# Score products in three steps, and an exp in two bf16 tiles that VectorE multiplies

## The chip, the cores and the metric

The kernel runs on one core of one Trainium2 chip. The metric is device microseconds of one execution. The profile is of one more execution, with every instruction's start and duration. Engines are named as the profile names them: PE is TensorE's matmul, PEld its weight load, ACT is ScalarE, DVE is VectorE, POOL is GpSimd, SP is SyncE, whose queue issues nearly all DMAs.

## The reference

For x of 2048 tokens by 1024 channels, a gate mixes a linear state space model with an attention block:

```
g = sigmoid((x * gate_w).sum(-1))
a: Bu = x @ B_bar.T (complex);  h_t = Lam_bar * h_(t-1) + Bu_t;  y = 2 * Re(h @ C.T) + x * Dskip
b: q, k, v of 32 heads of 32;  softmax(q k' / sqrt(32)) v;  @ wo
out = g * a + (1 - g) * b        # bf16 in and out
```

The attention has 32 x 2048 x 2048 scores, and each needs an exponential.

## The kernel before, in words

**Bursts.** The 32 heads are taken four at a time, as 8 groups. A group has 8 units of 256 queries, a unit 8 bursts of 256 keys: 512 bursts. In a burst (`burst`, L1612) PE computes eight score products, for two key tiles (`kl`) and four heads (`h`), each 32 rows by 256 queries (L1624). They go into two of three PSUM slots, which rotate: slot `sl[0]` holds heads 0 and 1, `sl[1]` heads 2 and 3. ScalarE takes the exp of each slot, 128x1024, as one instruction (`exp`, L1643). PE then multiplies exps of the burst before by V (`pv`, L1709), and adds up to about four 512-column products of a "dense chain": projections to Q, K and V (L1426, L1445), the products with B called u (L1457), with C (L1504), and the output projection (L1535). All dense chains end in PSUM bank 7, and VectorE copies the result out (`evac`) before the next one writes there.

**Order.** It is written out beforehand. `build` (L1734) steps through the bursts and keeps a clock of its own: a burst is given `PERIOD` = 1.83 us, 0.17 less after one with a shortened exp, and VectorE's clock `dve_t` is advanced by a planned cost for each operation. VectorE's other work, the state space scan and its tables and folds (`bg`, `bg2`), is put in where it fits in front of a limit. Each engine then works through its own list in that order and waits on semaphores. A `Sched.op` with `writes` waits for all readers and writers of its token; one with `acc` waits for those on other engines only, and becomes the token's last writer.

**X tiles.** ScalarE is relieved in 92 pairs of bursts (`X_PLAN`, `X_AT`). In a burst of a pair, the last 256 columns of the second slot are not given to ScalarE, whose exp is then 128x768 (L1640). VectorE copies them from PSUM, scaled, as 32-bit fixed point numbers (`x_in`, L1633); the short exp waits for it, since both read the slot. After the pair's second x_in come the steps of `x_ops` (L1653) on 128x512: `lo`, the low 16 bits, is the fraction of the exponent, `hi` the whole part. VectorE does two polynomial steps (L1667, L1668) and a third that adds `hi` (L1664); GpSimd then scales that to the bits of a bf16 (L1665), and PE multiplies it by V (`x_pv`, L1688). `X_LAST` is both the planned cost of the third step and the mark by which the planner knows it. `x_flush` runs what is left of the steps when PE's product comes due.

**Weights.** `wb` holds Q's weights once, K's and V's for two groups in turn (`w_of`), three B tiles, and late in the run some rows of the output weights. `build` issues Q's load at burst 28 of a group, K's and V's, for the group after the next, at burst 25. The C matrix comes in as transposing DMAs from burst `C_LOADS` on, every fourth burst.

Of the kernel before, what the change touches and what calls it, by code (L numbers as in the profile page):

```python
# [6 lines left out]
BF = mybir.dt.bfloat16  # L7
# [3 lines left out]
ALU = mybir.AluOpType  # L11
# [720 lines left out]
class GpPhaseA:  # L732
# [24 lines left out]
    def first(self, name):  # L757
        return self.alias.pop(name, [])
# [164 lines left out]
GROUPS = 8  # L923
# [8 lines left out]
RING = 60  # L932
C_LOADS = 28

X_AT = ((0, 2), (4, 6), (0, 4))
X_PLAN = (64, 72, 80, 88, 92, 96, 100, 104, 108, 112, 116, 120, 124, 128, 132, 136, 144, 152, 160, 168, 172, 176, 180, 184, 188, 192, 200, 208, 216, 224, 228, 232, 236, 240, 244, 248, 252, 256, 260, 264, 272, 280, 288, 296, 304, 312, 316, 320, 324, 328, 332, 336, 344, 352, 356, 360, 364, 368, 372, 376, 380, 384, 388, 392, 396, 400, 404, 408, 412, 416, 420, 424, 428, 432, 436, 440, 444, 448, 452, 456, 460, 464, 468, 472, 476, 480, 484, 488, 492, 496, 500, 504)
X_COLS = 256
F_TS, F_ST = 1.32, 1.24
I_MM = 0.61
X_LAST = 0.735  # L940
U_LAG, U_AHEAD = 3, 32
# [17 lines left out]
class FastPath:  # L959

    def __init__(self, nc, S, es, d, flag):
# [10 lines left out]
        self.V = T("V", [128, 2, 16, 4, 33], BF)  # L972
        wb = T("wb", [128, 8192], BF)
        self.wq = wb[:, 0:1024].rearrange("p (a n) -> p a n", a=8)
        self.wkv = wb[:, 1024:5120].rearrange("p (s q a n) -> p s q a n", s=2, q=2, a=8)
        self.bT = wb[:, 5120:8192].rearrange("p (s a n) -> p s a n", s=3, a=8)

        row = lambda o, n: wb[:, o:o + 1024 * n].rearrange("p (a n) -> p a n", a=n)
        self.wo3 = [row(1024, 2), row(5120, 3), row(3072, 1), self.cT[0][:, 0:1, :], self.cT[0][:, 1:2, :]]
        self.wo = [(self.wo3[0][:, a, :], "wo0") for a in range(2)] + [(self.wo3[4][:, 0, :], "wo4")] + [(self.wo3[1][:, a, :], "wo1") for a in range(3)]  # L980
        self.wo += [(self.wo3[3][:, 0, :], "wo3"), (self.wo3[2][:, 0, :], "wo2")]
        self.pt = T("pt", [128, 6, 2, 512], BF)
# [3 lines left out]
        self.hp = hp  # L986
        self.hpx = wb[:, 5120:8192].rearrange("p (k n) -> p k n", k=6)
        ub = T("ub", [128, 2, 2, 512], BF)
# [3 lines left out]
        self.xq = T("xq", [128, 2 * X_COLS], F32)  # L992
        self.xp = T("xp", [128, 2 * X_COLS], BF)
        self.ut = T("ut", [128, 2, 512], F32)
        self.ht = T("ht", [128, 2, 512], BF)
# [69 lines left out]
    def w_of(self, g, part):  # L1065
        return (self.wkv[:, g % 2, part - 1], ("w", g % 2, part)) if part else (self.wq, ("w", 0, 0))

# [544 lines left out]
    def burst(self, B):  # L1612
# [5 lines left out]

        def mm(e):
            m = None  # L1620
            for kl in range(2):
                for h in range(4):
                    kt = 2 * i + kl
                    m = e.matmul(ps[:, 2 * sl[h // 2] + h % 2, 256 * kl:256 * (kl + 1)], K[32 * h:32 * h + 32, g % 2, 128 * kt:128 * (kt + 1)],  # L1624
                                 Q[32 * h:32 * h + 32, qz, qo:qo + 256], start=True, stop=True, tile_position=(32 * h, 0))
# [27 lines left out]
    def x_ops(self, b):  # L1653

        xi, xq, xp = self.xi[:, b % 2], self.xq, self.xp
        lo = xi.bitcast(mybir.dt.uint16)[:, 0::2]
        hi = xi.bitcast(mybir.dt.int16)[:, 1::2]
        bits = xp.bitcast(mybir.dt.int16)[:]
        w = 65536.0
        i2, p2 = [("xi", b % 2, 0), ("xi", b % 2, 1)], [("xp", 0), ("xp", 1)]  # L1660

        def last():
            assert self.x_out == len(self.x_done)
            self.dve(lambda e: e.scalar_tensor_tensor(xq[:], hi, 128.0 / X_K, xq[:], ALU.mult, ALU.add), i2 + ["xq"], ["xq"], "x_q")  # L1664
            self.pool(lambda e: e.tensor_scalar(bits, xq[:], X_K, 128.0 * (E0 + 126.0), ALU.mult, ALU.add), ["xq"], p2, "x_p")  # L1665
            self.x_done.add(b)
        return [(0.73, 0.0, lambda: self.dve(lambda e: e.scalar_tensor_tensor(xq[:], lo, E2 / E3 * w, lo, ALU.add, ALU.mult), i2, ["xq"], "x_q")),  # L1667
                (0.73, 0.0, lambda: self.dve(lambda e: e.scalar_tensor_tensor(xq[:], xq[:], E1 / E3 * w * w, lo, ALU.add, ALU.mult), ["xq"] + i2, ["xq"], "x_q")),  # L1668
                (X_LAST, 0.0, last)]
# [64 lines left out]
    def build(self):  # L1734
# [8 lines left out]
        for m in range(3):  # L1743
            self.ld_b(m)
        for part in (1, 2):
            self.ld_w(1, part)
        self.plan()
        self.pt_own = {}
        self.x_of, self.x_batch, self.x_when = {}, [], {}
        self.xbg, self.x_done, self.x_out = [], set(), 0  # L1750
        self.opening()
# [32 lines left out]
        first = FIRST  # L1784
        wo1 = wo6 = last = False
        nal = nc = 0
# [3 lines left out]
        for p in range(first, NBURST):  # L1790
# [40 lines left out]

            if pg == 25 and g + 2 < GROUPS:
                assert g or not (proj[0] or cur and cur.tag == "proj")
                for part in (1, 2):
                    self.ld_w(g + 2, part)
            if pg == 28 and g + 1 < GROUPS:
                assert not (cur and cur.tag == "proj")
                self.ld_w(g + 1, 0)
            wsv = self.d["B_wo"].rearrange("(a p) n -> p a n", p=128)
            if p == 386:  # L1840
                self.dma(lambda e: e.dma_start(self.wo3[0], wsv[:, 0:2, :]), [], ["wo0"] + [("w", 0, q) for q in (1, 2)], "ld_wo")
            if not cs and cur is None and not wo1 and self.c_left[3] == 0:
                wo1 = True
                self.dma(lambda e: e.dma_start(self.wo3[1], wsv[:, 3:6, :]), [], ["wo1"] + [("bT", r) for r in range(3)] + [("hp", 8, k) for k in range(6)], "ld_wo")
            if g >= 6 and not wo6 and not cs and self.c_left[3] == 0:
                wo6 = True
                self.dma(lambda e: e.dma_start(self.wo3[3], wsv[:, 6:7, :]), [], ["wo3", ("cT", 0, 0), ("cTf", 0, 0, 0), ("cTf", 0, 0, 1)], "ld_wo")
                self.dma(lambda e: e.dma_start(self.wo3[4], wsv[:, 2:3, :]), [], ["wo4", ("cT", 0, 1), ("cTf", 0, 1, 0), ("cTf", 0, 1, 1)], "ld_wo")
            if g >= 6 and not last and not proj[7] and not us and not cs and cur is None and not self.bg:

                last = True
                xs = [("xr", r) for r in range(16)]
                assert wo1 and wo6
                self.dma(lambda e: e.dma_start(self.wo3[2], wsv[:, 7:8, :]), [], ["wo2"] + [("w", 1, q) for q in (1, 2)] + xs, "ld_wo")
            if g >= 6 and not cs and self.c_left[3] == 0 and nal < 8 and p > self.c_end:
# [50 lines left out]
            while self.xbg or self.bg or self.bg2:  # L1906
# [40 lines left out]
                if c > 0:  # L1947
                    self.dve_t = now + c
            if ended is not None:
                ended.evac()  # L1950
                self.dve_t = max(self.dve_t, dense_end) + 0.65
# [4 lines left out]
    def tail(self):  # L1956
# [41 lines left out]
        for r in range(2):  # L1998
            for cb in range(2):
                bank = 2 + r + 2 * cb  # L2000
                w = dict(acc=[("tb", bank)]) if cb == 0 else dict(writes=[("tb", bank)] + ([("S", 2)] if r == 0 else []), **({} if r == 0 else dict(acc=[("S", 2)])))
                S.op("pe", lambda e, r=r, cb=cb, bank=bank: e.matmul(ps[:, bank, :], OT[:, 7, 1792 + 128 * r:1920 + 128 * r], wo[7][0][:, 512 * cb:512 * (cb + 1)],
                                                                    start=(cb == 1), stop=True), reads=[("OT", 7, 7, r), "wo2"], name="tail", **w)
            if r == 0:
# [131 lines left out]
```

## Time and profile before

| | |
|---|---|
| median of 3 runs | 926.67 us (926.38 to 930.31) |
| the profiled execution | 928.11 us, its span from first to last instruction 926.3 us |
| granted TensorE clock, mean | 0.996 |
| busy, of the span | PE 902.5, ACT 907.3, DVE 758.4, POOL 86.8 us |
| full exps, short exps | 840, 184 |
| DMA | 77.69 MB, mean 84 GB/s |

A group of the profile reads: line, engine, operation, out<-in by the program's names, shapes, count | busy us, mean ns of one | idle time just before, and what ended it. A row of the timeline reads: start, duration, engine, line, operation, count, and in brackets the idle time before it with its releaser. A row of the stretches gives busy time of PE, PEld, DVE, ACT and POOL with counts, then clock, DMA share and GB/s. A row of the waits gives the total, the number and the longest. Consecutive operations of an engine can overlap: the next one's start can lie before the end of the one before.

### The profile page before, as it was taken

Reading aid. Unit: us, or ns where it says so; the run is one execution under the profiler, and the core shown is the slowest. Engines: PE = TensorE matmul, PEld = TensorE weight load, DVE = VectorE, ACT = ScalarE, POOL = GpSimd, SP = SyncE. Lnnn points to the kernel's source line nnn. Section 1 sums busy time; section 2 is a strip of 40 time slices with the busy share of each in tenths; the row PEclk is TensorE's granted clock in tenths of the full one; section 3 lists DMA queues with packets and bytes.
Section 4 is the critical chain, followed back from the end, with each engine's and each line's share of the span. In section 5 each row is a group of like instructions: output and inputs, shape, how many; then the busy total and the mean of one; then the engine's idle time right before and its main releaser. Section 6 shows DMA issues by size and latency. Waiting matters only on the chain.

```text
span 926.3 us, 33979 instructions
## 1 busy us (share of the span) xinstructions
PE 902.5 (97%) x15316; PEld 503.9 (54%) x15316; DVE 758.4 (82%) x1310; ACT 907.3 (98%) x1034; POOL 86.8 (9%) x156
## 2 busy tenths in 40 slices
PE   8899999999999999999999999999999999999996
PEld 4554754557555565546655565555655655445553
DVE  2788989998989999989989999899988655776665
ACT  6999999999999999999999999999999999999996
POOL 2000000111000101011111020000010010001010
PEclk9999999999999999999999999999999999999998
DMA  9569747750457101272012511413001112424312
GB/s 195 87 116 184 93 84 138 144 116 5 81 113 152 50 20 49 67 147 53 19 51 65 126 45 31 104 63 103 20 15 43 31 51 77 156 83 128 114 62 75
DMA packets 170934, 77.69 MB, mean 84 GB/s; under 512 B 147232, under 2 KB 155424, under 8 KB 170784
## 3 DMA queue, kind: packets, MB, share of 16 engines
q1 hardware_dynamic: 168624, 74.94, 36.3%
q8 instruction: 121, 1.98, 0.9%
q10 hardware_dynamic: 2160, 0.53, 0.3%
q14 instruction: 29, 0.24, 0.1%
HBM read 25.18 MB, written 20.97 MB: 50 GB/s over the span
## 4 chain that ended last, share of the span: by engine, by line
PE 52%; ACT 40%; DVE 4%; DMA 2%; SPq 1%; issue 1%; POOL 0%; DVEq 0%; ACTq 0%
ACT f_pt L1643 32%; PE f_ps L1709 14%; PE f_ps L1624 10%; PE f_ps L1426 9%; PE f_ps L1504 7%; PE f_ps L1457 6%; ACT f_pt L1640 5%; PE f_ps L1445 5%; SPq L1062 1%; ACT f_cT L1643 1%; PE f_ps L1688 1%; DMA f_xT<-in_A_x_dram 1%; ACT f_Et L1643 1%; DMA f_wb<-in_A_B_im_dram 1%; DMA f_ub<-u_scratch 0%
## 5 line engine op out<-in xcount | busy, mean ns | idle before, releaser
L1643 ACT ACTIVATE f_pt<-f_ps 128x1024 bf16<-128x1024 f32 x760 | 728.8, 1090 | 1.5 <-PE f_ps L1624 1.3
L1709 PEld LDWEIGHTS f_ps<-f_V,f_pt 128*128 128x128 bf16 x7184 | 222.2, 96 | 95.3 <-issue 68.7
L1709 PE MATMUL f_ps<-f_V,f_pt 128*128 128x33 bf16 x7184 | 258.0, 178 | 0.0
L1624 PE MATMUL f_ps<-f_Q,f_K 32*128 32x256 bf16 x4096 | 203.3, 273 | 10.8 <-ACT f_pt L1643 3.3
L1640 ACT ACTIVATE f_pt<-f_ps 128x768 bf16<-128x768 f32 x184 | 165.3, 898 | 0.7 <-PE f_ps L1624 0.6
L1624 PEld LDWEIGHTS f_ps<-f_Q,f_K 32*128 32x128 bf16 x4096 | 60.7, 92 | 148.0 <-ACT f_pt L1643 120.6
L1457 PE MATMUL f_ps<-f_xT,f_wb 128*128 128x512 bf16 x512 | 131.5, 379 | 1.6 <-DMA f_wb<-in_A_B_im_dram 0.7
L1665 POOL TENSOR_SCALAR f_xp<-f_xq 128x512 int16<-128x512 f32 x92 | 67.3, 732 | 646.0 <-DVE f_xq L1664 471.3
L1426 PE MATMUL f_ps<-f_xT,f_wb 128*128 128x512 bf16 x464 | 119.3, 379 | 0.1
L1633 DVE TENSOR_SCALAR f_xi<-f_ps 128x256 int32<-128x256 f32 x184 | 77.4, 421 | 17.6 <-PE f_ps L1624 13.3
L1362 DVE TENSOR_TENSOR_SCAN f_ht<-f_pf,f_init,f_ut 128x512 bf16<-128x512 f32 x64 | 81.3, 1279 | 0.0
L1504 PE MATMUL f_ps<-f_cT,f_hp 128*128 128x512 bf16 x272 | 74.5, 379 | 0.1
L1667 DVE SCALAR_TENSOR_TENSOR f_xq<-f_xi 128x512 f32<-128x512 uint16 x92 | 63.7, 692 | 3.2
L1668 DVE SCALAR_TENSOR_TENSOR f_xq<-f_xq,f_xi 128x512 f32<-128x512 f32 x92 | 63.6, 692 | 3.1
L1664 DVE SCALAR_TENSOR_TENSOR f_xq<-f_xi,f_xq 128x512 f32<-128x512 int16 x92 | 63.5, 690 | 2.6
L1457 PEld LDWEIGHTS f_ps<-f_xT,f_wb 128*128 128x128 bf16 x512 | 40.1, 96 | 40.5 <-issue 8.6
L1535 PE MATMUL f_ps<-f_wb,f_OT 128*128 128x512 bf16 x188 | 61.2, 381 | 0.4 <-DVE f_Et L1547 0.4
L1445 PE MATMUL f_ps<-f_wb,f_xT 128*128 128x128 bf16 x896 | 59.3, 219 | 0.0
L1426 PEld LDWEIGHTS f_ps<-f_xT,f_wb 128*128 128x128 bf16 x464 | 36.1, 96 | 35.6 <-issue 7.6
L1461 DVE CAST f_ub<-f_ps 128x512 bf16<-128x512 f32 x64 | 44.1, 688 | 10.4 <-PE f_ps L1457 9.7
L1445 PEld LDWEIGHTS f_ps<-f_wb,f_xT 128*128 128x128 bf16 x896 | 50.4, 97 | 3.8 <-issue 3.8
L1722 DVE RECIPROCAL f_rc<-f_ps 128x8 f32<-128x8 f32 x63 | 13.1, 207 | 47.6 <-PE f_ps L1688 43.5
(149 smaller groups left out, 822.5 us busy)
## 6 DMA issues: line engine op xcount, KB each, us to landing
u_scratch<-f_ub SPq DMA_DIRECT2D x64, 128.0 KB, 2.1
f_ub<-u_scratch SPq DMA_DIRECT2D x32, 256.0 KB, 3.0
ag_scratch<-f_Ag SPq DMA_DIRECT2D x32, 256.0 KB, 2.0
f_hp<-ag_scratch SPq DMA_DIRECT2D x32, 256.0 KB, 3.0
f_wb<-in_B_wqkv_dram SPq DMA_DIRECT2D x21, 256.0 KB, 4.1
out_dram<-f_xT SPq DMA_DIRECT2D x16, 256.0 KB, 2.2
f_OT<-f_On SPq DMA_TRANSPOSE x63, 2.3
f_wb<-in_B_wo_dram SPq DMA_DIRECT2D x1, 768.0 KB
```

The lines of the kernel that those rows point to most:

```text
L1362: ops.append((1.24, lambda ri=ri: dve(lambda e: e.tensor_tensor_scan(ht[:, ri, :], rr, ut[:, ri, :], self.init[:, ri, j:j + 1], ALU.mult, ...
L1426: mms.append((1, lambda e, f, l, a=a, w=w: e.matmul(ps[:, bank, :], w[:, a, :], xT[:, a, 512 * ch:512 * (ch + 1)], start=f, stop=l), [tok] ...
L1445: m = e.matmul(ps[:, bank, 128 * q:128 * (q + 1)], xT[:, a, 128 * kt:128 * (kt + 1)], w[:, a, :], start=(a == 0), stop=(a == 7))
L1457: mms.append((1, lambda e, f, l, a=a: e.matmul(ps[:, 7, :], bT[:, (2 * n + ri) % 3, a, :], xT[:, a, 512 * ch:512 * (ch + 1)], start=f, sto ...
L1504: mms.append((1, lambda e, f, l, j=j, ri=ri, h=h: e.matmul(ps[:, 7, :], h[:, cols], cT[ri][:, j, 512 * cb:512 * (cb + 1)], start=f, stop=l ...
L1624: m = e.matmul(ps[:, 2 * sl[h // 2] + h % 2, 256 * kl:256 * (kl + 1)], K[32 * h:32 * h + 32, g % 2, 128 * kt:128 * (kt + 1)], Q[32 * h:32 ...
L1633: first = self.dve(lambda e: e.tensor_scalar(self.xi[:, b % 2, X_COLS * n:X_COLS * (n + 1)], ps[:, 2 * s + 1, 512 - X_COLS:512], X_A, X_LO ...
L1640: self.S.op("act", lambda e: e.activation(flat(self.tile[p]), flat(ps[:, 2 * s:2 * s + 2, :]), ACT.Exp, scale=SCALE), reads=[("S", s)], wr ...
L1643: self.act(lambda e: e.activation(self.tile[p], ps[:, 2 * s:2 * s + 2, :], ACT.Exp, scale=SCALE), [("S", s)], [("pt", p)], "exp")
L1665: self.pool(lambda e: e.tensor_scalar(bits, xq[:], X_K, 128.0 * (E0 + 126.0), ALU.mult, ALU.add), ["xq"], p2, "x_p")
L1667: return [(0.73, 0.0, lambda: self.dve(lambda e: e.scalar_tensor_tensor(xq[:], lo, E2 / E3 * w, lo, ALU.add, ALU.mult), i2, ["xq"], "x_q") ...
L1709: m = e.matmul(ps[:, 6, o:o + 33], self.tile[p][:, h2, 256 * kl + 128 * qt:256 * kl + 128 * (qt + 1)], V[:, g % 2, 2 * i + kl, h, :], star ...
```

## The change

- The eight score products of a burst become three operations of PE: two products that write the first slot, four that end the first slot and begin the second, two that end the second. The order of the products stays.
- `x_ops`: VectorE's third step goes. GpSimd makes two bf16 tiles, `xe` (two to the whole part, from `hi`) beside the first step and `xm` (the polynomial's value) after the second; VectorE multiplies them into `xp`. The multiplication is planned at 0.36 and not before 0.9 us (`X_GAP`) after the step before it.
- The list of pairs loses 92 and 100 and gains 268, 276, 284, 292, 300 and 308: 96 pairs.
- K's and V's weights have one buffer each; K's and V's for the next group are loaded at a group's first burst (K's for group 1 at burst 17), Q's at burst 38 (`W_AT`). Projections may start four bursts later.
- C is loaded from burst 32 on. The output weights go to rows of the C and B tiles, seven loads at once when the C chains are done, and the last row later.

```diff
-C_LOADS = 28
+C_LOADS = 32
+W_AT = (38, 0, 17)
-X_LAST = 0.735
+X_LAST = 0.36
-X_K = 128.0 * E3 / 65536.0 ** 3
+X_K = E3 / 65536.0 ** 3
+X_GAP = 0.9
...
+        self.wqkv = [wb[:, 1024 * k:1024 * (k + 1)].rearrange("p (a n) -> p a n", a=8) for k in range(3)]
...
-        def mm(e):
+        def mm(e, some):
...
-        self.S.op("pe", mm, reads=[("K", g % 2, i // 2), ("Q", qz)], writes=[("S", sl[0]), ("S", sl[1])], name="qk")
+        s0, s1 = ("S", sl[0]), ("S", sl[1])
+        for some, kw in ((((0, 0), (0, 1)), dict(writes=[s0])),
+                         (((0, 2), (0, 3), (1, 0), (1, 1)), dict(writes=[s1], acc=[s0])),
+                         (((1, 2), (1, 3)), dict(acc=[s1]))):
+            self.S.op("pe", lambda e, some=some: mm(e, some), reads=[("K", g % 2, i // 2), ("Q", qz)], name="qk", **kw)
...
+        def first():
+            self.dve(lambda e: e.scalar_tensor_tensor(xq[:], lo, E2 / E3 * w, lo, ALU.add, ALU.mult), i2, ["xq"], "x_q")
+            self.pool(lambda e: e.tensor_scalar(bits, hi, 128.0, 128.0 * 127.0, ALU.mult, ALU.add), i2, ["xe"], "x_e")
+
+        def second():
+            self.dve(lambda e: e.scalar_tensor_tensor(xq[:], xq[:], E1 / E3 * w * w, lo, ALU.add, ALU.mult), ["xq"] + i2, ["xq"], "x_q")
+            self.pool(lambda e: e.tensor_scalar(self.xm[:], xq[:], X_K, E0, ALU.mult, ALU.add), ["xq"], ["xm"], "x_m")
+
         def last():
-            self.dve(lambda e: e.scalar_tensor_tensor(xq[:], hi, 128.0 / X_K, xq[:], ALU.mult, ALU.add), i2 + ["xq"], ["xq"], "x_q")
-            self.pool(lambda e: e.tensor_scalar(bits, xq[:], X_K, 128.0 * (E0 + 126.0), ALU.mult, ALU.add), ["xq"], p2, "x_p")
+            self.dve(lambda e: e.tensor_tensor(xp[:], self.xm[:], self.xe[:], ALU.mult), ["xm", "xe"], p2, "x_p")
...
-                proj[g][8 + c].after = max(16 * c, 32)
+                proj[g][c].after = W_AT[1] + 4
+                proj[g][8 + c].after = max(16 * c, W_AT[0] + 4)
...
-            if pg == 25 and g + 2 < GROUPS:
-                for part in (1, 2):
-                    self.ld_w(g + 2, part)
-            if pg == 28 and g + 1 < GROUPS:
+            if pg == W_AT[1 if g else 2] and g + 1 < GROUPS:
+                self.ld_w(g + 1, 1)
+                if g:
+                    self.ld_w(g + 1, 2)
+            if pg == W_AT[0] and g + 1 < GROUPS:
                 self.ld_w(g + 1, 0)
...
-                    if c == X_LAST and self.x_out != len(self.x_done):
+                    if c == X_LAST and (xs or now < self.x_ready or self.x_out != len(self.x_done)):
...
+                if i:
+                    self.x_ready = self.dve_t + X_GAP
```

More of the change, by code (lines that the diff above doesn't have):

```diff
@@ L1065, in w_of @@
     def w_of(self, g, part):
-        return (self.wkv[:, g % 2, part - 1], ("w", g % 2, part)) if part else (self.wq, ("w", 0, 0))
+        return self.wqkv[part], ("w", 0, part)
     def ld_w(self, g, part, eng="sp"):
@@ L1617, in burst @@
         qz, qo = (4 * g + qb // 2) % 5, 256 * (qb % 2)
-        def mm(e):
+        def mm(e, some):
             m = None
[L1621 to L1625, printed above, removed]
-            return m
-        self.S.op("pe", mm, reads=[("K", g % 2, i // 2), ("Q", qz)], writes=[("S", sl[0]), ("S", sl[1])], name="qk")
+            for kl, h in some:
+                kt = 2 * i + kl
+                m = e.matmul(ps[:, 2 * sl[h // 2] + h % 2, 256 * kl:256 * (kl + 1)], K[32 * h:32 * h + 32, g % 2, 128 * kt:128 * (kt + 1)],
+                             Q[32 * h:32 * h + 32, qz, qo:qo + 256], start=True, stop=True, tile_position=(32 * h, 0))
+            return m
+        s0, s1 = ("S", sl[0]), ("S", sl[1])
[3 more added lines that the diff above has]
+            self.S.op("pe", lambda e, some=some: mm(e, some), reads=[("K", g % 2, i // 2), ("Q", qz)], name="qk", **kw)
         mine = self.x_of.get(B)
@@ L1744, in build @@
             self.ld_b(m)
-        for part in (1, 2):
-            self.ld_w(1, part)
+        self.ld_w(1, 2)
         self.plan()
@@ L1784, in build @@
         first = FIRST
-        wo1 = wo6 = last = False
+        wo1 = last = False
         nal = nc = 0
@@ L1838, in build @@
+            if pg == W_AT[0] and g + 1 < GROUPS:
+                assert not proj[0]
                 self.ld_w(g + 1, 0)
             wsv = self.d["B_wo"].rearrange("(a p) n -> p a n", p=128)
-            if p == 386:
-                self.dma(lambda e: e.dma_start(self.wo3[0], wsv[:, 0:2, :]), [], ["wo0"] + [("w", 0, q) for q in (1, 2)], "ld_wo")
-            if not cs and cur is None and not wo1 and self.c_left[3] == 0:
+            if not wo1 and not cs and cur is None and self.c_left[3] == 0:
@@ L1843, in build @@
                 wo1 = True
[L1844 to L1848, printed above, removed]
+                for a in range(7):
+                    j = a if a < 3 else a - 3
+                    x = [("cT", 0, j), ("cTf", 0, j, 0), ("cTf", 0, j, 1)]
+                    if a in (3, 4, 5):
+                        x = [("bT", a - 3)] + [("hp", 8, k) for k in (2 * a - 6, 2 * a - 5)]
+                    self.dma(lambda e, a=a: e.dma_start(self.wo[a][0], wsv[:, a, :]), [], ["wo%d" % a] + x, "ld_wo")
@@ L1849, in build @@
             if g >= 6 and not last and not proj[7] and not us and not cs and cur is None and not self.bg:
                 last = True
-                xs = [("xr", r) for r in range(16)]
-                assert wo1 and wo6
-                self.dma(lambda e: e.dma_start(self.wo3[2], wsv[:, 7:8, :]), [], ["wo2"] + [("w", 1, q) for q in (1, 2)] + xs, "ld_wo")
+                assert wo1
+                self.dma(lambda e: e.dma_start(self.wo[7][0], wsv[:, 7, :]), [], ["wo7", ("cT", 0, 4), ("cTf", 0, 4, 0), ("cTf", 0, 4, 1)], "ld_wo")
```

32 lines of the change are left out of this document (14 added, 18 removed).

## The prediction, made before the result was known

> **What bounds the kernel now.** I read the page first, then the stretches, the chain of waits, and last the timeline around single pairs.
>
> ```profile
> span 926.3 us, 33979 instructions
> PE 902.5 (97%) x15316; PEld 503.9 (54%) x15316; DVE 758.4 (82%) x1310; ACT 907.3 (98%) x1034; POOL 86.8 (9%) x156
> ```
>
> PE at 97% and ACT at 98% look alike. A PE row counts matmuls whose ends are modelled, so ACT has to be asked separately: is it ever without work?
>
> ```profile
> 25.00:900.00 875.00, 864.26 (x14833) 483.22 (x14826) 737.19 (x1244) 871.79 (x991) 80.76 (x132) 1.00 0.36 81
> 650.00:675.00 25.00, 25.00 (x495) 17.21 (x494) 22.88 (x40) 25.00 (x30) 2.47 (x4) 1.00 0.07 18
> ```
>
> The columns are PE, PEld, DVE, ACT and POOL busy time. Between 25 and 900 us ACT is idle for 875 - 871.79 = 3.2 us in all. So ACT carries the time, and anything that doesn't shorten its own work can return only little. The chain of waits shows its beat:
>
> ```profile
> 258.69 6.42 ACT f_pt L1643 x7
> 265.11 0.70 ACT f_pt L1640
> L1643 ACT ACTIVATE f_pt<-f_ps x760: 1018/1103/1309, 9.9 to 916.1; 128x1024 bf16<-128x1024 f32 x190
> L1640 ACT ACTIVATE f_pt<-f_ps 128x768 bf16<-128x768 f32 x184 | 165.3, 898 | 0.7 <-PE f_ps L1624 0.6
> ```
>
> Seven full exps take 6.42 us, 0.917 each; one shortened by an x tile takes 0.70. (Each lasts over 1 us, since the next starts before it ends.) The first exp starts at 9.9 and the last at 916.1, 906.2 us apart. The 1024 exps, 184 of them short, need 839 x 0.917 + 184 x 0.70 = 898.2 between those starts. So 8.0 us are lost to waits of every kind: 3.2 as idle ACT after 25 us, and an estimated 4.8 in the opening and in starts late by less than the overlap. Those 8.0 are all that the score step, DVE and the DMAs could give back.
>
> **Four more pairs.** 92 pairs become 96, so eight exps shrink from 0.917 to 0.70: 8 x 0.217 = **-1.7 us**. This lies on the path and is the surest term.
>
> **Score products in three steps.** Today all eight wait until both slots are free:
>
> ```profile
> PEld f_ps L1624 <- ACT f_pt L1643: 120.6, 312, 1.0
> 402.67 0.12 PEld L1624 LDWEIGHTS f_ps<-f_Q,f_K 32*128 32x128 bf16 x8 [0.42 <-ACT f_pt L1643]
> 402.68 0.40 PE L1624 MATMUL f_ps<-f_Q,f_K 32*128 32x256 bf16 x8
> L1624 PE MATMUL f_ps<-f_Q,f_K x4096: 264/268/278, 9.5 to 914.7; 32*128 32x256 bf16 x196
> ```
>
> One product lasts 0.268 and eight 0.40, so they run as two rounds of four, 0.13 apart. The first step needs only slot 0, which the exp before last left. It can run ahead of ACT, and then the second step holds the two others of the first round beside the first two of the next. The first exp is released after the sixth product, not the eighth: at best 0.13 earlier. That counts only in bursts where PE stood waiting for ACT (312), and there ACT has work in hand anyway; what helps is that PE starts its values and dense products 0.13 sooner, and the next burst is less often late. Where PE arrives late by itself nothing changes. Bounds: 0 (ACT is covered) and half of the 4.8, 2.4. I take a quarter, **-1.2 us**, since much of the 4.8 stands in the opening, where PE is behind. A gain is not excluded by any row, and neither is a small loss for one more wait per burst; no row prices that, so I put it at nothing, covered by the same 0.13.
>
> **Weights and C later.** The one large idle stretch of ACT is this:
>
> ```profile
> 65.46 1.29 SPq L1081 DMA_TRANSPOSE f_cT<-in_A_C_re_dram  x1
> 66.79 1.30 SPq L1081 DMA_TRANSPOSE f_cT<-in_A_C_im_dram  x1
> 68.14 1.28 SPq L1071 DMA_DIRECT2D f_wb<-in_B_wqkv_dram  x1
> 69.53 0.67 SPq L1474 DMA_DIRECT2D f_ub<-u_scratch  x1
> 73.34 0.69 DVE L1353 TENSOR_TENSOR f_ht<-f_ub,f_Et 128x1024 bf16<-128x1024 bf16 x1 [2.39 <-DMA f_ub<-u_scratch]
> 75.27 0.57 PE L1709 MATMUL f_ps<-f_V,f_OT 128*128 128x33 bf16 x16 [1.24 <-DVE f_On L1723]
> 77.36 1.94 ACT L1643 ACTIVATE f_OT<-f_ps 128x1024 bf16<-128x1024 f32 x2 [1.34 <-PE f_ps L1624]
> ```
>
> Burst 28 issues the first pair of C transposes and Q's weights. Both stand ahead of the load of u at 69.53; VectorE sits 2.39 us for it, PE waits 1.24 for the normalisation queued behind on VectorE, and ACT loses 1.34. The change moves C to burst 32 and Q's weights to 38, so the load has a free queue. A later load of u then meets C instead, where VectorE may have other work or not. Bounds 0 and -1.34; I take **-0.8**.
>
> K's and V's weights have one buffer now and are loaded at a group's first burst (K for group 1 at burst 17).
>
> ```profile
> f_wb<-in_B_wqkv_dram SPq DMA_DIRECT2D x21, 256.0 KB, 4.1
> ```
>
> They land in 4.1 us, and no product may use them for four bursts, at least 4 x 1.62 = 6.5 us by the exps above (one full, one short). SP then holds u's stores and B's transposes behind two loads instead of at burst 25: the same queueing at another place, nothing net. If the cover went, a dense chain would wait perhaps 1 us, seven times at most. The output weights become seven single loads at one moment and an eighth later; the output chains still start at burst 442 at the earliest, behind the last projections, so nothing.
>
> **VectorE and GpSimd.** Per pair the third VectorE pass over 512 float32 elements goes, and a bf16 product comes. GpSimd does two passes instead of one: the exponent tile as soon as the pair's second x_in is done, the mantissa tile after the second VectorE pass.
>
> ```profile
> 292.26 0.42 DVE L1633 TENSOR_SCALAR f_xi<-f_ps 128x256 int32<-128x256 f32 x1
> 292.72 0.69 DVE L1667 SCALAR_TENSOR_TENSOR f_xq<-f_xi 128x512 f32<-128x512 uint16 x1
> 293.44 0.69 DVE L1668 SCALAR_TENSOR_TENSOR f_xq<-f_xq,f_xi 128x512 f32<-128x512 f32 x1
> 402.84 0.42 DVE L1353 TENSOR_TENSOR f_Ag<-f_tq,f_ut 128x512 bf16<-128x512 bf16 x1
> 296.17 0.68 DVE L1664 SCALAR_TENSOR_TENSOR f_xq<-f_xi,f_xq 128x512 f32<-128x512 int16 x1
> 296.76 0.69 DVE L1353 TENSOR_TENSOR f_ht<-f_ub,f_Et 128x1024 bf16<-128x1024 bf16 x1
> 296.93 1.00 POOL L1665 TENSOR_SCALAR f_xp<-f_xq 128x512 int16<-128x512 f32 x1 [15.61 <-DVE f_xq L1664]
> 297.37 1.10 DVE L1353 TENSOR_TENSOR f_tq<-f_ub,f_Et 128x1024 bf16<-128x1024 bf16 x1
> L1665 POOL TENSOR_SCALAR f_xp<-f_xq x92: 617/618/1590, 140.9 to 909.1; 128x512 int16<-128x512 f32 x92
> ```
>
> By durations alone VectorE saves 0.68 - 0.42 = 0.26 a pair, 24 us over 92 pairs, and spends 4 x (2 x 0.42 + 2 x 0.69 + 0.42) = 10.6 on the new four. But the rows from 296.17 on show a price. A GpSimd pass takes 0.62 alone; begun inside a VectorE operation with two SBUF inputs it took 1.00, ended 0.48 after that operation, and the next VectorE operation took 1.10 instead of 0.69: 0.41 lost. In the kernel before, the GpSimd pass comes late in a pair, often beside work on PSUM, and the median is the undisturbed 0.618. The exponent pass will not have that: it is released when x_in ends, exactly when the first pass starts (292.26, 292.72), which reads two SBUF operands, with the second right behind. So I expect the second pass to grow by 0.41 in nearly every pair: 96 x 0.41 = 39 us of VectorE, more than the 24 saved.
>
> The Trainium skill, "SBUF — State Buffer", section "SBUF: two separate sides", has this as a rule: VectorE with two SBUF inputs and GpSimd exclude each other for a whole instruction, and whoever starts first blocks the other fully. By the rule the second pass would wait out a whole undisturbed GpSimd pass, 0.62, and the 39 us would be 60; the trace agrees on who blocks whom, and its 0.41 decides the size.
>
> The mantissa pass is released after the second pass, followed by any scan operation that the planner has. It blocks only if two such operations follow in a row; where an evacuation from PSUM comes second, it costs nothing. The multiplication is planned 0.9 after the second pass, and an undisturbed GpSimd pass is done after 0.08 + 0.62, a disturbed one after 0.08 + 1.00, so VectorE may stand 0.2 for it; behind it then stand x_in, evacuations and normalisations.
>
> VectorE is off the path until it delays x_in, for which the short exp waits:
>
> ```profile
> 404.49 0.40 PE L1624 MATMUL f_ps<-f_Q,f_K 32*128 32x256 bf16 x8
> 404.94 0.42 DVE L1633 TENSOR_SCALAR f_xi<-f_ps 128x256 int32<-128x256 f32 x1
> 405.99 0.98 ACT L1640 ACTIVATE f_pt<-f_ps 128x768 bf16<-128x768 f32 x1
> 822.02 0.40 PE L1624 MATMUL f_ps<-f_Q,f_K 32*128 32x256 bf16 x8
> 823.85 0.42 DVE L1633 TENSOR_SCALAR f_xi<-f_ps 128x256 int32<-128x256 f32 x1
> 824.36 0.81 ACT L1640 ACTIVATE f_pt<-f_ps 128x768 bf16<-128x768 f32 x1 [0.57 <-PE f_ps L1624]
> ```
>
> At 404.94 x_in starts as soon as the products end and is done 0.63 before the short exp starts. At 823.85 it came 1.4 us after its products, and ACT stood idle 0.57. So 0.41 alone is covered by 0.63, and costs only where VectorE was already some 0.35 late. Bounds: 0 and rival 1's figure. I take one pair in six, 16 x 0.12: **+2.0 us**.
>
> **The sum:** -1.7 - 1.2 - 0.8 + 2.0 = -1.7. The profiled execution took 928.11 (span 926.3) and would take 926.4; the median of the three runs, 926.67, stands 1.4 below it, so I predict 926.67 - 1.7 = **925.0**.
>
> **Rival 1: VectorE becomes the bound (slower).**
>
> ```profile
> 120.00:700.00 580.00, 576.02 (x9822) 321.51 (x9822) 523.22 (x836) 579.22 (x661) 62.20 (x100) 1.00 0.34 74
> 700.00:900.00 200.00, 197.52 (x3335) 107.23 (x3334) 134.46 (x260) 199.15 (x230) 17.30 (x29) 1.00 0.28 85
> ```
>
> VectorE is busy 523 of 580 us up to 700 and 134 of 200 after it. In 650 to 675 VectorE is idle 2.1 us of 25, which hold 3.5 pairs at four bursts each: 0.6 a pair. If both GpSimd passes cost 0.41, each pair asks 0.82; the planner doesn't know of it and fills the saved time with scan work. Above 0.6 a pair the lateness accumulates, and ACT pays about 0.2 a pair. Of the 96 pairs 65 lie in the first six groups, up to about 690 us: 13 us, and 926.67 - 3.7 + 13 = 936, with 928 to 942 by how many mantissa passes are hit. For it: the scan work never runs out before 700. Against: an evacuation often stands second after a pair, and normalisation leaves gaps.
>
> **Rival 2: it all comes back (faster).** VectorE absorbs the lock, PE's head start returns 2.2 and u's load 1.3: -5.2, **921.5**. For it: x_in has 0.63 of cover. Against: ACT's idle after 25 us is just 3.2.
>
> **Rival 3: the head start is void.** PE is mostly still streaming the dense products when the exp ends (97% busy), so the early pair of products finds no gap: -1.7 - 0.8 + 2.0, **926.2**.
>
> **How the numbers follow.** My forecast 0.42, rival 1 0.29, rival 2 0.17, rival 3 0.12. A measurement can tell about 0.5%, here 4.6 us: 922.0 to 931.3 counts as the same. Faster: two thirds of rival 2, 0.11. Slower: two thirds of rival 1, 0.19. Same: the rest, 0.70. The range 921 to 934 leaves out the upper part of rival 1 (0.12) and a little below rival 2 (0.05). The forecast's own range is 923 to 928.
>
> **What would show it.** 192 short exps and ACT busy for about 1.7 us less; GpSimd's 192 passes, the exponent ones near 1.0 to 1.2, the second VectorE pass near 1.1 instead of 0.69; PE's wait for ACT before the score products split between their first and third product; no gap of 1.34 near 77 us. I am wrong if the second pass stays at 0.69 (no lock: rival 2), if ACT's idle between 120 and 700 us grows from 0.8 beyond 5 us with waits on x_in (rival 1), or if PE's dense products wait for weights at a group's start.

## The result, and the profile after

The changed kernel takes 933.24 us (median of 6, 932.84 to 935.45), the kernel before on the same chip 926.55 (median of 6). The ratio is 1.0062, interval 1.0048 to 1.0077: slower, where 925.0 was predicted. It lies inside the range of 921 to 934, near the upper end. The page of the changed kernel, profiled at 933.03:

```profile
span 931.2 us, 33811 instructions
PE 884.7 (95%) x15095; PEld 511.0 (55%) x15316; DVE 764.3 (82%) x1330; ACT 909.2 (98%) x1034; POOL 217.4 (23%) x256
...
L1670 POOL TENSOR_SCALAR f_xe<-f_xi 128x512 int16<-128x512 int16 x96 | 107.5, 1120 | 470.5 <-DVE f_xi L1639 470.5
L1646 ACT ACTIVATE f_pt<-f_ps 128x768 bf16<-128x768 f32 x192 | 169.3, 882 | 0.9 <-PE f_ps L1626 0.5
...
L1674 POOL TENSOR_SCALAR f_xm<-f_xq 128x512 bf16<-128x512 f32 x96 | 88.7, 924 | 60.2 <-DVE f_xq L1673 60.2
...
L1673 DVE SCALAR_TENSOR_TENSOR f_xq<-f_xq,f_xi 128x512 f32<-128x512 f32 x96 | 93.8, 977 | 3.2
...
L1669 DVE SCALAR_TENSOR_TENSOR f_xq<-f_xi 128x512 f32<-128x512 uint16 x96 | 66.5, 692 | 3.3
```

The page has 192 short exps and 2 x 96 GpSimd passes. 221 of 15316 matmul records are missing from this trace, nearly all of them one product of a dense chain each (15095 of PE stand against 15316 of PEld), so PE's busy time isn't compared, and below the waits in front of dense chains are read from PEld, the weight loads. The exponent pass takes 1.120 and the second VectorE pass 0.977, against 0.69 before. The total of VectorE hardly tells anything, 764 us against 758. The stretches (PE, PEld, DVE, ACT, POOL busy, clock, DMA share, GB/s) say where the time went:

```profile
25.00:900.00 875.00, 842.12 (x14509) 486.33 (x14721) 740.03 (x1256) 867.74 (x984) 208.49 (x229) 1.00 0.34 81
120.00:700.00 580.00, 555.25 (x9553) 321.26 (x9692) 522.84 (x845) 574.11 (x652) 156.67 (x168) 1.00 0.32 74
700.00:900.00 200.00, 195.79 (x3276) 109.41 (x3322) 135.57 (x261) 198.84 (x229) 50.54 (x57) 1.00 0.29 88
```

ACT is idle 5.9 us between 120 and 700, where it was 0.8, and 1.2 after 700, where it was 0.85. Taking every exp's end to the next one's end, less 0.917 or 0.70, counts starts that are late by less than the overlap too: before lost 7.8 us in all, after 15.0, of which more than 10 lie between 120 and 700 us, where before lost about 2. The short exps save their 1.7, so the sum is +5.5; the two profiled executions are 4.9 apart. Of the 15.0, some 13 are lost in front of exps that waited for PE's score products (about 80 of them), and only 1.3 in front of short exps that waited for x_in (10). What PE's weight loads waited for, in the waits of after (total, number, longest), with two rows of other engines:

```profile
ACT f_pt L1649 <- PE f_ps L1626: 5.7, 19, 0.6
...
PEld f_ps L1507 <- DVE f_Ag L1520: 3.1, 7, 0.8
...
PEld f_ps L1429 <- DVE f_Q L1436: 2.2, 5, 0.7
...
PEld f_ps L1429 <- DVE f_Ag L1520: 1.4, 2, 0.7
...
PEld f_ps L1429 <- DVE f_K L1436: 1.4, 4, 0.6
DVE f_xp L1678 <- POOL f_xm L1674: 1.3, 3, 0.4
...
PEld f_ps L1448 <- DVE f_V L1454: 0.9, 4, 0.3
```

The five PEld waits come to 9.0 us. In before, the same chains have two such waits of 0.2. L1507, L1429 and L1448 are the products of dense chains, and what their first weight load waits for is VectorE's copy of bank 7 (L1520, L1436, L1454). A stricter count agrees: from 100 to 900 us, the time in which neither a matmul nor a weight load ran and which ended at a dense chain within 0.2 us of such a copy's end is 8.8 us in after and 0.8 in before. PE works through its list in order, so behind the waiting chain stand the next score products, and behind those ACT. VectorE's multiplication had to wait for the mantissa pass in only 3 pairs, 1.3 us, so the longer GpSimd work does not itself explain the loss. One pair shows it from end to end. First VectorE alone, in its timeline of after, then the others in the full timeline of the same stretch:

```profile
306.75 0.42 DVE L1639 TENSOR_SCALAR f_xi<-f_ps 128x256 int32<-128x256 f32 x1
307.21 0.69 DVE L1669 SCALAR_TENSOR_TENSOR f_xq<-f_xi 128x512 f32<-128x512 uint16 x1
307.94 0.98 DVE L1673 SCALAR_TENSOR_TENSOR f_xq<-f_xq,f_xi 128x512 f32<-128x512 f32 x1
308.84 1.69 DVE L1356 TENSOR_TENSOR f_ut<-f_ht,f_tq 128x512 f32<-128x512 bf16 x2
310.46 0.74 DVE L1520 TENSOR_SCALAR f_Ag<-f_ps,f_gcol 128x512 f32<-128x512 f32 x1
```

```profile
307.26 1.12 POOL L1670 TENSOR_SCALAR f_xe<-f_xi 128x512 int16<-128x512 int16 x1 [5.76 <-DVE f_xi L1639]
...
309.00 1.00 POOL L1674 TENSOR_SCALAR f_xm<-f_xq 128x512 bf16<-128x512 f32 x1 [0.62 <-DVE f_xq L1673]
...
309.07 0.38 PE L1507 MATMUL f_ps<-f_cT,f_hp 128*128 128x512 bf16 x1
...
311.25 0.55 PEld L1429 LDWEIGHTS f_ps<-f_xT,f_wb 128*128 128x128 bf16 x4 [0.73 <-DVE f_Ag L1520]
...
312.22 0.40 PE L1626 MATMUL f_ps<-f_Q,f_K 32*128 32x256 bf16 x8
...
312.65 2.85 ACT L1649 ACTIVATE f_pt<-f_ps 128x1024 bf16<-128x1024 f32 x3 [0.42 <-PE f_ps L1626]
```

From x_in's start to the copy's are 3.71 us. The C chain's last product ended at 309.45; the copy starts 1.0 later, the weight load of PE's next chain stands 0.73 for it, and ACT loses 0.42. The same pair where GpSimd's passes read no SBUF (`both_fill`, below) stands beside it:

```profile
305.05 0.42 DVE L1639 TENSOR_SCALAR f_xi<-f_ps 128x256 int32<-128x256 f32 x1
305.51 0.69 DVE L1669 SCALAR_TENSOR_TENSOR f_xq<-f_xi 128x512 f32<-128x512 uint16 x1
306.24 0.69 DVE L1673 SCALAR_TENSOR_TENSOR f_xq<-f_xq,f_xi 128x512 f32<-128x512 f32 x1
306.85 1.29 DVE L1356 TENSOR_TENSOR f_ut<-f_ht,f_tq 128x512 f32<-128x512 bf16 x2
308.05 0.75 DVE L1520 TENSOR_SCALAR f_Ag<-f_ps,f_gcol 128x512 f32<-128x512 f32 x1
```

3.00 us from x_in to the copy, and PE's next chain (L1429) begins at 308.85 with no wait. The 0.71 between them is 0.29 on the second pass and 0.42 on the two adds in which the mantissa pass began (1.69 against 1.29, and the start 0.02 off). That is one pair, and a bad one; over all 96 the operations of VectorE lost 34 us in after beyond their usual durations (0.36 a pair), 27 of them in the second pass and the rest in 19 other operations, against 4.7 us in before.

### The profile page after: what moved, and what is told of

The parts are those of the page before. It is cut to its first block, busy times and chain, and to the rows that moved or that the text cites. A ratio compares the mean times of both kernels' runs of the same rounds, so it can differ in the third digit from the quotient of the medians.

```text
span 931.2 us, 33811 instructions
## 1 busy us (share of the span) xinstructions
PE 884.7 (95%) x15095; PEld 511.0 (55%) x15316; DVE 764.3 (82%) x1330; ACT 909.2 (98%) x1034; POOL 217.4 (23%) x256
## 4 chain that ended last, share of the span: by engine, by line
PE 62%; DVE 20%; ACT 13%; issue 4%; DMA 1%; POOL 0%; DVEq 0%; SPq 0%
PE f_ps L1721 14%; PE f_ps L1626 12%; PE f_ps L1460 10%; PE f_ps L1507 9%; PE f_ps L1429 8%; ACT f_pt L1649 8%; PE f_ps L1448 5%; DVE f_xi L1639 3%; DVE f_xq L1669 3%; DVE f_ht L1365 2%; DVE f_xq L1673 2%; ACT f_pt L1646 2%; DVE f_ut L1356 2%; DVE f_Ag L1520 2%; DVE f_ub L1464 1%
## 5 line engine op out<-in xcount | busy, mean ns | idle before, releaser
L1626 PE MATMUL f_ps<-f_Q,f_K 32*128 32x256 bf16 x4096 | 214.2, 273 | 5.0 <-ACT f_pt L1649 2.0
L1670 POOL TENSOR_SCALAR f_xe<-f_xi 128x512 int16<-128x512 int16 x96 | 107.5, 1120 | 470.5 <-DVE f_xi L1639 470.5
L1646 ACT ACTIVATE f_pt<-f_ps 128x768 bf16<-128x768 f32 x192 | 169.3, 882 | 0.9 <-PE f_ps L1626 0.5
L1626 PEld LDWEIGHTS f_ps<-f_Q,f_K 32*128 32x128 bf16 x4096 | 67.5, 92 | 139.0 <-ACT f_pt L1649 88.3
L1460 PE MATMUL f_ps<-f_xT,f_wb 128*128 128x512 bf16 x448 | 117.7, 379 | 10.7 <-DVE f_xi L1639 3.3
L1429 PE MATMUL f_ps<-f_xT,f_wb 128*128 128x512 bf16 x406 | 106.7, 379 | 9.8 <-DVE f_Q L1436 2.8
L1674 POOL TENSOR_SCALAR f_xm<-f_xq 128x512 bf16<-128x512 f32 x96 | 88.7, 924 | 60.2 <-DVE f_xq L1673 60.2
L1673 DVE SCALAR_TENSOR_TENSOR f_xq<-f_xq,f_xi 128x512 f32<-128x512 f32 x96 | 93.8, 977 | 3.2
L1507 PE MATMUL f_ps<-f_cT,f_hp 128*128 128x512 bf16 x240 | 67.6, 379 | 5.6 <-DVE f_Ag L1520 3.6
L1448 PE MATMUL f_ps<-f_wb,f_xT 128*128 128x128 bf16 x896 | 59.3, 219 | 0.5 <-DVE f_V L1454 0.2
L1429 PEld LDWEIGHTS f_ps<-f_xT,f_wb 128*128 128x128 bf16 x464 | 36.1, 96 | 40.3 <-issue 7.6
L1448 PEld LDWEIGHTS f_ps<-f_wb,f_xT 128*128 128x128 bf16 x896 | 50.3, 98 | 4.7 <-issue 3.8
L1368 POOL CAST f_hl<-f_ht 128x2 f32<-128x2 bf16 x24 | 11.1, 461 | 156.6 <-DVE f_ht L1365 156.3
```

Of the source, the lines that this page charges most:

```text
L1429: mms.append((1, lambda e, f, l, a=a, w=w: e.matmul(ps[:, bank, :], w[:, a, :], xT[:, a, 512 * ch:512 * (ch + 1)], start=f, stop=l), [tok] ...
L1448: m = e.matmul(ps[:, bank, 128 * q:128 * (q + 1)], xT[:, a, 128 * kt:128 * (kt + 1)], w[:, a, :], start=(a == 0), stop=(a == 7))
L1460: mms.append((1, lambda e, f, l, a=a: e.matmul(ps[:, 7, :], bT[:, (2 * n + ri) % 3, a, :], xT[:, a, 512 * ch:512 * (ch + 1)], start=f, sto ...
L1507: mms.append((1, lambda e, f, l, j=j, ri=ri, h=h: e.matmul(ps[:, 7, :], h[:, cols], cT[ri][:, j, 512 * cb:512 * (cb + 1)], start=f, stop=l ...
L1646: self.S.op("act", lambda e: e.activation(flat(self.tile[p]), flat(ps[:, 2 * s:2 * s + 2, :]), ACT.Exp, scale=SCALE), reads=[("S", s)], wr ...
L1670: self.pool(lambda e: e.tensor_scalar(bits, hi, 128.0, 128.0 * 127.0, ALU.mult, ALU.add), i2, ["xe"], "x_e")
```

## The experiments

Ratios are to the kernel before, from runs on the same chip. Its median was 928.55, 928.68 and 928.24 us in the three sets of experiments, but 926.55 beside the changed kernel. The expectations name times against 926.5, so times of the experiments are read by their ratios, and a difference between the changed kernel and an experiment is uncertain by up to 2 us. The first four kernels take the change apart: its score products alone, its loads alone, all but the two tiles (with before's 92 pairs), and the two tiles with the loads (92 pairs, score products in one step; without the loads' smaller `wb` the tiles have no room).

**`split_only`.**

```diff
 # before, with only
-        self.S.op("pe", mm, ..., writes=[("S", sl[0]), ("S", sl[1])], name="qk")
+        # two products write slot 0, four end it and begin slot 1, two end slot 1
```

> The kernel before with the score products in three steps and nothing else of the change. Theory A (the two GpSimd tiles make VectorE late, bank 7 is copied out late, and PE's next dense chain and score products with it): the split itself is harmless or helps; 924.5 to 926.5 us against 926.5 before. Theory B (three steps cost PE more than they return: more waits and signals on the engine that the score products share with all else): 929 or more. Theory C (the later, single-buffered weight loads hold up dense chains): as before, 926.

Measured: 929.37 us, 0.9999 (0.9982 to 1.0015). Theory B's 929 is met by the number alone: before took 928.55 beside it. The split neither gains nor costs. PE's waits for ACT before the score products do shrink, in the waits:

```profile
PEld f_ps L1623 <- ACT f_pt L1646: 85.7, 237, 0.7
```

It was 120.6 us before, yet nothing arrives. Measured from the end of the exp that frees the later slot, in bursts where PE waited for it, the eight products started at 0.06 (four) and 0.18 (four) in before. In the split kernel the first two started anywhere from 0.09 ahead of that end to 0.07 behind it, but the last two again at 0.18: they start where the last four did, since heads 2 and 3 still need two rounds after that exp, and PE's next work begins 0.38 after it in both kernels. Only the first exp of the burst is released earlier, at a time when ACT still has the other slot in hand.

**`loads_only`** and, in a later set, **`c_late`**, one constant of it.

```diff
 # loads_only: before, with
-C_LOADS = 28
+C_LOADS = 32
+W_AT = (38, 0, 17)     # and the smaller wb, the other load times, the output weights' rows
 # c_late: before, with
-C_LOADS = 28
+C_LOADS = 32
```

> The kernel before with the weight, C and output-weight loads moved as in the change, and nothing else. Theory A: 925 to 926.5 us; the stall of 1.3 us near 77 us goes. Theory B: the same. Theory C: 929 or more, with PE waiting for DMAs of weights at the start of groups.

> The kernel before with one number changed: C is loaded from burst 32 on, not 28. If the gain of the moved loads (0.32%) comes from the load of u that stood behind the first C transposes near 70 us, this alone brings most of it: 925.5 to 927 us, and ACT's lost time in bursts 32 to 63 falls from over 2 us to about 1. If it comes from the weights, no change, 928.

Measured: 925.95 us, 0.9968 (0.9955 to 0.9981), and 925.51 us, 0.9970 (0.9956 to 0.9984). Moving C behind u's load brings about 2.8 us, the whole gain of the loads as far as the intervals can tell. Q's weights still stood ahead of u's load in `c_late` (65.01 and 65.69), so they were not needed for it. The stretches of before, then of `c_late`:

```profile
60.00:85.00 25.00, 23.74 (x428) 12.44 (x427) 21.51 (x31) 23.66 (x27) 0.89 (x2) 1.00 0.92 171
```

```profile
60.00:85.00 25.00, 25.00 (x459) 13.33 (x459) 22.36 (x34) 25.00 (x28) 0.90 (x2) 1.00 0.92 166
```

**`no_tiles`** and **`tiles_and_loads`**.

```diff
 # no_tiles: after, with before's x_ops and its 92 pairs
 # tiles_and_loads: after, with before's 92 pairs and one operation for the eight products
```

> The changed kernel with the steps of a pair, and the 92 pairs, as before: split and loads without the two tiles. Theory A: 923 to 925.5 us, ACT's idle between 120 and 700 us under 1.5 us. Theories B or C: 930 or more.

> The kernel before with the two tiles and the loads, 92 pairs and the score products in one step (the two tiles need the room that the loads set free). Theory A: 932 to 936 us, the second VectorE pass near 0.98 us, PE's dense chains waiting on VectorE by 10 us or more between 120 and 700 us. Theory B: 926 or less. Theory C: between, 929 to 931, and no more than loads_only.

Measured: 926.42 us, 0.9977 (0.9966 to 0.9988), and 932.67 us, 1.0048 (1.0029 to 1.0066). So the loss comes in with the two tiles: from `loads_only` to `tiles_and_loads` the ratio rises by 0.0080, 7.4 us.

**`xe_fill`, `xm_fill`, `both_fill`** ask which GpSimd pass does it.

```diff
 # after, with
-            self.pool(lambda e: e.tensor_scalar(bits, hi, 128.0, 128.0 * 127.0, ALU.mult, ALU.add), i2, ["xe"], "x_e")
+            self.pool(lambda e: e.memset(self.xe[:], 1.0), i2, ["xe"], "x_e")                    # xe_fill, both_fill
-            self.pool(lambda e: e.tensor_scalar(self.xm[:], xq[:], X_K, E0, ALU.mult, ALU.add), ["xq"], ["xm"], "x_m")
+            self.pool(lambda e: e.memset(self.xm[:], 1.0), ["xq"], ["xm"], "x_m")                # xm_fill, both_fill
```

> The changed kernel, but GpSimd's exponent pass fills its tile with a constant and reads no SBUF (so the power of two is left out of the shortened exps); order, waits and planned costs stay. Theory A1 (the exponent pass takes the second VectorE pass's port): the second pass falls back from 0.98 to 0.69 us and the time by half of the tiles' 8 us or more, to 925 to 929. Theory A2 (the planner packs VectorE too full, since it now plans the multiplication at 0.36 and moves it behind the next x_in; the port is a side matter): 931 to 933.

> The changed kernel with both GpSimd passes as constant fills that read no SBUF (power of two and polynomial left out of the shortened exps); order and planned costs stay. Theory A1: no operation of VectorE is lengthened, PE no longer waits on VectorE's copies from bank 7, and the time is that of split and loads with 96 pairs, 922 to 925 us. Theory A2: 929 to 932.

> The changed kernel with the mantissa pass alone as a constant fill that reads no SBUF (the polynomial is left out of the shortened exps); the exponent pass stays. By theory A1 the second VectorE pass stays at 0.98 us and most of the loss with it: 928 to 931 us, against 925.9 where the exponent pass was the fill.

Measured: `xe_fill` 925.89 us, 0.9972 (0.9963 to 0.9981); `xm_fill` 927.11, 0.9987 (0.9976 to 0.9998); `both_fill` 923.0, 0.9944 (0.9931 to 0.9958). The second VectorE pass in the groups of `xe_fill`, then of `xm_fill`:

```profile
L1673 DVE SCALAR_TENSOR_TENSOR f_xq<-f_xq,f_xi 128x512 f32<-128x512 f32 x96 | 66.4, 692 | 3.2
```

```profile
L1673 DVE SCALAR_TENSOR_TENSOR f_xq<-f_xq,f_xi 128x512 f32<-128x512 f32 x96 | 93.7, 976 | 3.2
```

A GpSimd pass that reads SBUF is what lengthens it, and one that only writes isn't; below, "the lock" is this hold of the one over the other. Against after's 933.24, taking either pass's lock away returns 6 to 8 us by medians and ratios, and taking both 10 to 11. So the two don't add: against `both_fill`, in the same order of work, the mantissa pass alone (`xe_fill`) costs about 0.0028, 2.6 us, the exponent pass alone (`xm_fill`) 0.0043, 4.0 us, and both together more than the sum. My expectation for `xm_fill`, 928 to 931, missed for that reason: I had put the loss on the exponent pass in proportion to its time, and most of the 28 us that VectorE loses in that kernel are covered. By the count above, PE stood for copies of bank 7 for 0.1 us in `both_fill`, 2.6 in `xe_fill` and 3.1 in `xm_fill`, against 8.8 in after.

**`after_90`** and **`true_cost_90`** keep both passes, and change what the planner is told.

```diff
 # after_90: after, without the six added pairs
 # true_cost_90: after_90, with
-        return [(0.73, 0.0, first), (0.73, 0.0, second), (X_LAST, 0.0, last)]
+        return [(0.73, 0.0, first), (1.02, 0.0, second), (X_LAST, 0.0, last)]
```

> The changed kernel without the six added pairs between bursts 268 and 308 (90 pairs): the control of the next. Six pairs less cost ACT 2.6 us and spare VectorE some 6 x 0.3 us of lengthened passes. Theory A1: 931 to 934 us. Theory A2: 929 to 932.

> As the control with 90 pairs, but the planner is told 1.02 us for the second VectorE pass instead of 0.73, which is what it takes in the trace. If the loss is lateness that the plan doesn't know of (both A1 and A2 say so, in part), scan work is laid elsewhere and PE waits less on VectorE: 926 to 930 us, and 3 us or more below the control. If VectorE's lengthened pass costs wherever it is put (no room left in the plan), within 1.5 us of the control.

Measured: 932.63 us, 1.0049 (1.0035 to 1.0063), and 926.52 us, 0.9978 (0.9969 to 0.9987). Six pairs more should bring 2.6 us by the exps; after, which has them, is no faster (1.0062), so these six cost at least what they save. And with the price in the plan 6.1 us come back, though the lock is still there, in the groups and the stretch of `true_cost_90`:

```profile
L1673 DVE SCALAR_TENSOR_TENSOR f_xq<-f_xq,f_xi 128x512 f32<-128x512 f32 x90 | 84.6, 940 | 2.7
120.00:700.00 580.00, 578.31 (x9802) 328.00 (x9798) 513.58 (x826) 579.21 (x660) 123.05 (x158) 1.00 0.33 75
```

ACT's idle time there is 0.8 us again, and PE stood 1.6 us for copies of bank 7, against 7.7 in `after_90`. Against `both_fill` and the 2.6 us of the six pairs (0.9944 + 0.0028), the lock costs 0.0077 in `after_90`, 7 us, and 0.0006 once it is planned, less than the intervals. One thing goes with it: another order also changes what the passes meet (the mantissa pass's mean is 0.71 here, 0.90 in `after_90`, and 78 of the 90 second passes are lengthened, not 89). VectorE still loses 30 us to lengthened operations, against 31 in `after_90`, so it is mainly the lateness against the plan and not the lengthening that costs; how much the other order does for itself isn't separated. With 92 or 96 pairs and the true price the written order has no room: scan work is left over when the output chains begin.

**`loads_94`** and **`loads_96`** ask whether before's x steps, which lock less, can carry more pairs.

```diff
 # loads_only, with
-X_LAST = 0.735
+X_LAST = 0.62         # loads_94: pairs 212 and 348 added; loads_96: X_LAST = 0.5 and after's 96 pairs
```

> The moved loads alone, with the pair's steps as before, the third step planned at 0.62 us instead of 0.735 (in the trace the next operation starts 0.60 after it) and two pairs more, at bursts 212 and 348. If the planned cost had room, four exps are 0.217 us shorter and nothing becomes late: 0.9 us below the moved loads alone, 924.5 to 925.5 us. If VectorE is full there, PE waits on its copies and the two pairs bring nothing or lose up to 2 us.

> The moved loads alone, with the pair's steps as before, the changed kernel's 96 pairs, and the third step planned at 0.50 us, 0.10 less than it takes: a small, known untruth in the plan, against 0.29 and more in the change. Theory A: 0.1 a pair is mostly covered, 923.5 to 926 us. If any overrun in the dense stretch counts in full: 926 to 929.

Measured: 925.83 us, 0.9975 (0.9963 to 0.9987), and 928.03, 0.9995 (0.9982 to 1.0008). Neither beats `loads_only`. The stretch of `loads_96` has VectorE at 91%, the highest of all kernels, and ACT idle 1.7:

```profile
120.00:700.00 580.00, 575.61 (x9813) 321.48 (x9808) 530.62 (x855) 578.27 (x660) 66.80 (x104) 1.00 0.33 75
```

The third pass lasts 0.69 there, with the next operation about 0.6 behind its start, and was planned at 0.5: again a price below the true one, in another operation and with no second GpSimd pass, and the eight shorter exps are more than paid back (0.9995 against 0.9968). PE stood 1.9 us for copies of bank 7, against 0.7 in `loads_only`. Whether the low price did it or a VectorE that is simply fuller, these two runs don't separate: `loads_94`, planned at 0.62, gains nothing either. Besides the two kernels of the loads alone, `no_tiles`, `loads_94` and `true_cost_90` lie below before with their whole intervals; `loads_only` and `c_late` have the lowest ratios of the kernels that leave nothing out, and none of the five can be told from the others.

## Why the prediction was wrong

The steps add up in ratios: loads -0.0032, split 0, four pairs -0.0018 (1.7 of 927), which makes 0.9950; `both_fill`, with the order of after and no lock, measured 0.9944. After stands at 1.0062, so the lock costs 0.0118, 10.9 us by the ratios and 10.2 by the medians. It outweighs the rest. (After and `both_fill` were measured in different sets, as said above.)

**The failed step is the term +2.0: "one pair in six, 16 x 0.12".** Its mechanism, a GpSimd pass that blocks VectorE's next operation with two SBUF inputs, was there, and it measured +10. Two things were wrong with the sizing. First, I asked only when x_in becomes late, found 0.63 of cover there, and let 0.41 vanish in it. Only 10 short exps waited for x_in, 1.3 us. The wait that ends first is another: the copy of bank 7, for which PE's next chain waits, with the next score products behind it. The mantissa pass, which the sum put at nothing, costs 2.6 us even alone. Second, I priced each pair by itself. The planner had put scan work into the time that it believed free, so nothing between two pairs took the lateness up, and it went on to the next copy. `true_cost_90` supports that, with the limit that its order differs.

**Rival 1**, VectorE as the bound, is nearest to what happened, and I had given it 0.29. Its price, 936 with 928 to 942, holds the measured 933.2. Its point of decision isn't borne out: the lock cost VectorE 0.36 a pair on average, well below the 0.6 of slack that I had read from the rows, and 0.71 only in a pair like the one shown, where the mantissa pass hit too. An average slack doesn't say whether a single copy comes late. Its wait was named wrongly, as the term's was. The argument against it, that "an evacuation often stands second after a pair", pointed at the place of the damage: the evacuation isn't lengthened itself, but it is what becomes late. My sign of error came true by half: ACT's idle time between 120 and 700 us grew beyond 5 us, but not "with waits on x_in".

**The size of the lock.** The second pass rose by 0.29 (0.98 in 95 of 96 pairs), not 0.41. The Trainium skill, "SBUF — State Buffer", section "SBUF: two separate sides", has the lock hold for the whole of the other's instruction, and only against a GpSimd operation that reads SBUF. The fills agree with the second half, 0.692 in `xe_fill` and `both_fill`. By my estimate from the first half the pass would have grown by 0.62; the measured 0.29 is less than half of that. The timeline shows why it is also below my row: the second pass follows 0.73 after the first one's start, because it needs its result, where the operations of that row followed 0.61 apart, and the GpSimd pass ends 0.48 after the first operation in both. The lengthened operation then ends 0.54 after GpSimd in both (308.92 and 308.38 in after, 298.47 and 297.93 in the row): the same hold, of which a later start feels less.

**Score products, -1.2: nothing.** The prediction asked when the first product starts; what matters to PE is when the last one does, and that isn't moved. Rival 3 put this term at nothing, as measured, but for another reason: PE did find the gap (its waits for ACT fell by 35 us), and the gap only moved.

**Loads, -0.8: right in kind, too small by over three.** The place and the cause hold, since C alone behind u's load brings 2.8. I had capped the gain at the 1.34 of the one profiled execution, and in the profiled execution of `split_only`, which has the same loads, the stall was longer, as the last section shows.

**Pairs, -1.7:** 192 short exps, as said; the sum above closes with it, but no run has the four pairs alone.

## What to carry to other kernels

In an order planned with fixed costs, an operation that is longer than its planned price can cost more than the same operation with its true price (7 us against under 1 here), since the plan has already given its slack away: price the interference, not only the durations. To ask what a late engine costs, go through everything that its list feeds, the copies that free a buffer above all, and take the first wait that has no cover left. A transfer that others queue behind may be worth more than one profile shows, if the stall it makes varies between executions.

## What the hardware showed unasked

**After a stall of PE the clock was halved for a while.** The profile of `split_only` caught it at the stall that C's early transposes make, in PE's and ACT's timeline and in its stretches:

```profile
72.46 1.02 PE L1457 MATMUL f_ps<-f_xT,f_wb 128*128 128x512 bf16 x4
73.42 0.40 PE L1623 MATMUL f_ps<-f_Q,f_K 32*128 32x256 bf16 x8
75.46 0.57 PE L1712 MATMUL f_ps<-f_V,f_OT 128*128 128x33 bf16 x16 [1.64 <-DVE f_On L1726]
75.87 0.25 PE L1712 MATMUL f_ps<-f_V,f_cT 128*128 128x33 bf16 x4
76.71 1.89 PE L1457 MATMUL f_ps<-f_xT,f_wb 128*128 128x512 bf16 x4 [0.58 <-DMA f_wb<-in_A_B_im_dram]
```

```profile
79.18 1.94 ACT L1646 ACTIVATE f_OT<-f_ps 128x1024 bf16<-128x1024 f32 x2 [3.39 <-PE f_ps L1623]
82.12 1.02 ACT L1646 ACTIVATE f_cT<-f_ps 128x1024 bf16<-128x1024 f32 x1 [1.00 <-PE f_ps L1623]
```

```profile
72.60:76.00 3.40, 1.76 (x33) 0.86 (x30) 2.44 (x6) 3.19 (x4) 0.00 (x0) 1.00 1.45 188
76.00:76.20 0.20, 0.13 (x5) 0.02 (x1) 0.20 (x1) 0.00 (x0) 0.00 (x0) 0.77 0.06 15
82.80:83.00 0.20, 0.20 (x2) 0.04 (x1) 0.20 (x2) 0.20 (x1) 0.00 (x0) 0.67 1.07 225
77.00:82.00 5.00, 5.00 (x44) 1.58 (x42) 2.30 (x3) 1.94 (x2) 0.00 (x0) 0.50 0.84 200
```

In the profile of before PE stood 1.24 us at this place, kept its clock, and ACT lost 1.34. Here PE stood 1.64; the granted clock fell to 0.50 at about 76.1 and stayed there to 82.9 us, PE stood another 0.58 right after the fall, four dense products took 1.89 instead of 1.02, and ACT lost 3.39 and 1.00. Together that is 3 us more than in before; how much of it is the clock and how much the second wait isn't separated. The Trainium skill, "TensorE: Matmul & The Clock Gate", section "What's actually happening", has the half rate after at least one idle window of about 3.4 us; in this trace PE had been busy 1.76 of the 3.40 us before the fall, with no idle stretch longer than 1.64, and the half rate lasted 6.8. It may be part of what spreads the runs of before: of 85 further ones, 37 had a mean clock of 0.995 or lower and took 930.0 us on average, the other 48 took 927.7. That their clock fell at this place isn't shown, since only `split_only`'s execution was profiled in it, and a low mean has another source too: the profile of `no_tiles` has a mean of 0.993 with the full clock here, because its clock stood at 0.50 over the last 13 us.

**A GpSimd fill doesn't disturb VectorE**, and it is itself even: 0.52 us in `xe_fill` and `both_fill`, started beside the same two VectorE passes; the exponent pass, which reads SBUF, took 1.12 there.
